# Whole-height score products for the global queries, and one order of products for the values

## The chip, the cores and the metric

One core of a Trainium2 chip runs the whole program in one launch. The metric is device time in microseconds (us) of one execution; lower is better. The core's engines run side by side and meet through semaphores: TensorE (in the rows PE for products, PEld for its weight loads), VectorE (DVE), ScalarE (ACT), GpSimd (POOL) and the SyncE queue (SP) that issues all the transfers here.

## The reference

```
k_all = concat([k_g, k_l]); v_all = concat([v_g, v_l])       # 4 batches, 8 heads, 32 + 512 tokens, 64 wide
out_g = softmax(q_g @ k_all.T / 8) @ v_all                   # 32 global queries see every key
s_ll  = where(|pos_i - pos_j| <= 32, q_l @ k_l.T / 8, -1e9)  # 512 local queries see a band ...
s_lg  = q_l @ k_g.T / 8                                      # ... and the 32 global keys
out_l = softmax(concat([s_lg, s_ll])) @ concat([v_g, v_l])
x = tokens of concat([out_g, out_l]), 2176 x 512
x = relu(x @ w_in)**2 @ w_out                                # d_ff 2048
h = x @ w2_in;  x = P(h) / Q(h) @ w2_out                     # P cubic, Q = 1 + |b0||h| + |b1|h*h
```

## The kernel before

The program has an attention stage (about the first 143 us) and then two feed-forward blocks, in one hand-written order (`tc.manual_schedule`): each engine carries out its instructions in the order in which the code lists them, and waits where a semaphore is not there yet.

Two heads make a pair, so there are 16 pairs. The first head's 64 values of q and k lie on partitions 0 to 63, the second's on 64 to 127. The loop over `p` (lines 488 to 586) is a pipeline: in iteration `p` TensorE does the scores of pair p, the transposes of pair p-1, and the products with the values of pairs p-2 and p-1. Each iteration has two halves of the same kind (u = 0 and 1; 256 local queries each):

- `scores(p, u)`, L299: eight products of 64 by 64 weights with 160 keys into the banks `s_ps[2u]` and `s_ps[2u+1]`, one bank for each head.
- `maxima`, L308 on VectorE, reads a bank, adds the mask and takes the row maximum; only then can that bank be written again. `exps`, L316 on ScalarE; `sums`, L320, and the reciprocal of `norm`, L324, on VectorE; the four scalings of `norm`, L327, on GpSimd.
- `transp`, L345 and L346: five transposes by TensorE, which need the scalings of GpSimd; `transp_evac`, L350 on ScalarE and L352 on VectorE, copies them out as `p1` (local keys) and `p2` (global keys).
- `pv(p, u)`, lines 354 to 383: the products with the values, in one bank `pv_ps[u]`. `glob(i)`, L370, multiplies `p2` by a 128 by 128 block that holds the global values of both heads. `win`, L364, multiplies the local probabilities of one window by 128 by 64 values, once for each head, whose results lie on partitions 0 to 63 and 64 to 127. For u = 1, L382 adds the last keys of the global queries. `pv_local` and `pv_global` (L389, L396, L398) copy the bank out.

In every second iteration `g_scores(g)`, L413 and L414, makes the scores of the global queries of four heads (two pairs, one of them a pair ahead). For each head it writes 32 partitions of bank c1 (`s_ps[0]`, 512 columns) and of bank c2 (`s_ps[1]`, 64 columns), from the head's 64 partitions of q and k. The first call uses the banks `tc_ps`. `g_transp`, L443 and L444, transposes the result an iteration later.

A product of fp32 values stands in the trace as two records, one for each pass over the columns; a transpose as one.

While this goes on, VectorE also prepares the feed-forward weights, four steps per 128 by 512 chunk (L101, L103, L105, L108) and a cast, L117, and GpSimd subtracts, L125. From iteration 3 on, each has one chunk. Transfers wait in one queue; q and k have four buffers, so pair p+3 is asked for once pair p-1's scores are done.

Of the kernel before, what the change touches and what calls it, by code (L numbers as in the profile page):

```python
# [11 lines left out]
F32 = mybir.dt.float32  # L12
# [9 lines left out]
B, H, SL, SG, D = 4, 8, 512, 32, 64  # L22
DM, DFF = 512, 2048
NTOK = B * (SL + SG)
NB = SL // 128
NW = SL // 64
KW = 160
KE = 288
KL = 896
KC = KL + 288  # L30
VW = 4 * D
VG = VW * NW
VE = VG + 8 * D
# [15 lines left out]
def window(w):  # L49

    return KE + 80 * w if w % 2 == 0 else (0 if w < 4 else KL) + 80 * (w % 4 - 1)


def body(ctx, tc, qT, kW, v, w1i, w1o, w2i, w2o, coef, out):
    nc = tc.nc
    pe, act, dve, pool, sync = nc.tensor, nc.scalar, nc.vector, nc.gpsimd, nc.sync
# [178 lines left out]
    def ew2_b(s):  # L235
        n = TILES[(s // KF) % NT][1]
        a, b, t = pend.pop(s)
        dve.scalar_tensor_tensor(a, in0=a, scalar=EPS1, in1=b, op0=ALU.add, op1=ALU.mult)  # L238
        dve.scalar_tensor_tensor(t, in0=t, scalar=nf[:, 0:1], in1=b, op0=ALU.add, op1=ALU.mult)
        dve.scalar_tensor_tensor(t, in0=a, scalar=2.0, in1=t, op0=ALU.subtract, op1=ALU.mult)  # L240
        gh = ff_p["g"].tile([128, TW], F32R, tag="gh", name="gh")
        gl = ff_p["g"].tile([128, TW], F32R, tag="gl", name="gl")
        gs[s] = gh, gl
        return t, gh[:, :n], gl[:, :n]
# [8 lines left out]
    ident = msk_p.tile([128, 128], F32, name="ident")  # L253
    mask = msk_p.tile([128, NB, KW], F32, name="mask")
    v_p = att.enter_context(tc.tile_pool(name="v", bufs=2))
# [12 lines left out]
    qt, kt, vt = {}, {}, {}  # L268
    sm, pT, pgs, pgT = {}, {}, {}, {}

    def load_qk(p):
        b, hp = divmod(p, 4)
        qt[p] = qk_p.tile([128, SL + SG], F32, tag="q", name="q")
        kt[p] = qk_p.tile([128, KC], F32, tag="k", name="k")
        cuts = [(0, 0), (256, 576), (SL + SG, KC)] if p == 0 else [(0, 0), (SL + SG, KC)]
        for (q0, k0), (q1, k1) in zip(cuts, cuts[1:]):
            sync.dma_start(qt[p][:, q0:q1], qT[b, hp][:, q0:q1])
            sync.dma_start(kt[p][:, k0:k1], kW[b, hp][:, k0:k1])
# [8 lines left out]
    def sm_tiles(p, u):  # L287
        sm[p, u] = (sm_p.tile([128, 2 * KW, 2], F32, tag="sm", name="sm"),
                    st_p.tile([128, 4], F32, tag="nm", name="nm"),
                    st_p.tile([128, 4], F32, tag="sum", name="sum"),  # L290
                    st_p.tile([128, 4], F32, tag="rs", name="rs"))

    def scores(p, u):
        for i in range(2):
            for j in range(2):
                for a in range(2):
                    r, w = slice(64 * j, 64 * j + 64), 4 * u + 2 * i + (a if i else 1 - a)
                    c = window(w) - 32 * i
                    pe.matmul(s_ps[2 * u + j][64 * a:64 * a + 64, KW * i:KW * i + KW],  # L299
                              qt[p][r, 64 * w:64 * w + 64], kt[p][r, c:c + KW],  # L300
                              start=True, stop=True, tile_position=(64 * j, 64 * a))

    def maxima(p, u, j):
        s, nm = sm[p, u][:2]
        for i in range(2):
            b, k = 2 * u + i, 2 * j + i
            o = s[:, KW * i:KW * i + KW, j]
            dve.tensor_tensor_reduce(out=o, in0=s_ps[2 * u + j][:, KW * i:KW * i + KW], in1=mask[:, b],  # L308
                                     scale=-0.125, scalar=3.0e38, op0=ALU.add, op1=ALU.min,
# [44 lines left out]
    def pv(p, u):  # L354

        v = vt[p // 2]
        c = pgT[p // 2][1]
        p1, p2 = pT.pop((p, u))
        bank = pv_ps[u]

        def win(w, o0, o1, stop=False):
            for j in range(2):
                jj = 2 * (p % 2) + j
                pe.matmul(bank[64 * j:64 * j + 64, o0:o1], v[:, VW * w + 64 * jj:VW * w + 64 * jj + 64],  # L364
                          p1[:, j, o0 + (32 if o0 >= 128 else 0):o1 + (32 if o0 >= 128 else 0)],
                          start=False, stop=stop)

        def glob(i):
            o = VG + 256 * (p % 2) + 128 * i
            pe.matmul(bank[:, 160 * i:160 * i + 128], v[:, o:o + 128], p2, start=i == 1, stop=False)  # L370

        glob(1)
        win(4 * u, 64, 160)
        win(4 * u + 1, 0, 64)
        glob(0)
        win(4 * u + 2, 128, 224)
        win(4 * u + 3, 224, 288, stop=u == 0)
        if u:
            for j in range(2):
                jj = 2 * (p % 2) + j  # L380
                o = VE + 64 * jj
                pe.matmul(bank[64 * j:64 * j + 64, 128:160], v[0:64, o:o + 64], c[:, 32 * jj:32 * jj + 32],  # L382
                          start=False, stop=True)

    def pv_local(p, half):
        b, hp = divmod(p, 4)
# [15 lines left out]

    def g_scores(g):
        c1, c2 = s_ps[:2] if g else tc_ps
        for jj in range(4):
            p = 2 * g + jj // 2
            r = slice(64 * (jj % 2), 64 * (jj % 2) + 64)
            o = slice(32 * jj, 32 * jj + 32)
            even = kt[p][r, KE:KE + KW * NB].rearrange("p (a b) -> p a b", a=NB)[:, :, 0:128]
            last = kt[p][r, KC - 64:KC]  # L410
            last = bass.AP(tensor=last.tensor, offset=last.offset - (KC - 64 - KE - 128),
                           ap=[last.ap[0], [KC - 64 - KE - 128, 2], [1, 32]])
            pe.matmul(c1[o], qt[p][r, SL:], even, start=True, stop=True, tile_position=(64 * (jj % 2), 32 * jj))  # L413
            pe.matmul(c2[o, 0:64], qt[p][r, SL:], last, start=True, stop=True,  # L414
                      tile_position=(64 * (jj % 2), 32 * jj))
        m = st_p.tile([128, 8], F32, tag="gm", name="gm")
        dve.tensor_reduce(m[:, 0:1], c1[:, 32:], axis=AX.X, op=ALU.max)
        dve.tensor_reduce(m[:, 1:2], c2[:, 0:64], axis=AX.X, op=ALU.max)
        pgs[g] = pg[g % 2], m, c1, c2
# [29 lines left out]
    qk_p = qk_s.enter_context(tc.tile_pool(name="qk", bufs=4, side="right"))  # L449

    with tc.manual_schedule():
        act.preload_act_table_set("natural_log_exp_and_others")
        warm = raw_p.tile([128, 512], I64, tag="raw", name="raw").bitcast(BF16)[:, 0:512]
        dve.memset(warm, 0.0)
        load_qk(0)
        load_qk(1)
        load_qk(2)
        load_qk(3)
        load_v(0)
# [12 lines left out]
        for b, r, c in ((0, 64, 0), (2, 0, 0), (3, 64, 128)):  # L472
            o = 32 * (b % 2)
# [14 lines left out]
        for p in range(NP + 2):  # L488
# [14 lines left out]
            g = (p + 1) // 2  # L503
# [38 lines left out]
            if odd or p == 0:  # L542
                g_scores(g)
# [4 lines left out]
            if 2 <= p:  # L548
                pv(p - 2, 1)
# [27 lines left out]
            if pre:  # L577
                pv(p - 1, 0)
# [89 lines left out]
        for s in range(2, 2 * S1):  # L668
# [22 lines left out]
            if j == KF - 1:  # L691
                mm2(s - 2)
                mm2(s - 1)
                g = ew2_b(s) if s in pend else None
# [72 lines left out]
```

## Time and profile before

| | |
|---|---|
| median of 3 runs | 907.04 us (907.02 to 907.33) |
| the profiled execution | 906.48 us, its span 904.7 us |
| TensorE busy | 890.2 us, 98% of the span |
| TensorE weight loads busy | 783.4 us |
| VectorE, ScalarE, GpSimd busy | 662.7, 547.3, 258.8 us |
| chain that ended last | 86% of it TensorE, 10% VectorE |

The span is from the first to the last instruction; the time outside it is 1.8 us. An engine's busy time counts overlapping instructions once. Busy shares are means over stages that differ: in the attention stage all four engines are used, in the feed-forward blocks TensorE leads, but for a stretch at the start of the first block (to about 225 us) in which VectorE converts weights.

### The profile page before, as it was taken

How to read it: one execution, taken by the hardware profiler on the slowest of the kernel's cores; microseconds unless marked ns; L12 is line 12 of the kernel's file. 1: busy time of each engine (PE TensorE's matmuls, PEld its weight loads, DVE VectorE, ACT ScalarE, POOL GpSimd, SP SyncE). 2: the span in 40 equal slices, each digit the busy share in tenths (PEclk: the TensorE clock that was granted, in tenths of full speed). 3: DMA queues.
4: the chain of work that ended last, by engine and by line, in shares of the span. 5: the costliest groups of instructions: out<-in, count | busy, mean ns of one | idle time of the engine just before them, and what ended most of it. 6: DMA issues, size and time to landing. Idle time of an engine off the chain costs nothing.

```text
span 904.7 us, 14722 instructions
## 1 busy us (share of the span) xinstructions
PE 890.2 (98%) x5397; PEld 783.4 (87%) x5398; DVE 662.7 (73%) x1406; ACT 547.3 (60%) x1186; POOL 258.8 (29%) x324
## 2 busy tenths in 40 slices
PE   8999999997999999999999999999999999999998
PEld 4777778886888899999999978888888999999998
DVE  4788976999776568664332479877877888887886
ACT  5878874444433334342244568767766886886885
POOL 3667881334000000000036543221222222222221
PEclk9999999999999999999999999999999999999999
DMA  9767631333154327532014410001000100000001
GB/s 350 297 220 299 218 135 61 127 117 132 49 169 139 105 75 214 166 91 84 1 59 122 125 34 1 1 0 47 1 1 0 48 1 1 35 1 21 15 1 36
DMA packets 27576, 81.43 MB, mean 90 GB/s; under 512 B 3184, under 2 KB 4976, under 8 KB 26480
## 3 DMA queue, kind: packets, MB, share of 16 engines
q1 hardware_dynamic: 27504, 80.49, 26.3%
q8 instruction: 42, 0.69, 0.3%
q14 instruction: 30, 0.25, 0.1%
HBM read 67.64 MB, written 12.85 MB: 89 GB/s over the span
## 4 chain that ended last, share of the span: by engine, by line
PE 86%; DVE 10%; ACT 1%; issue 1%; DMA 1%; POOL 1%; SPq 0%; DVEq 0%; POOLq 0%; ACTq 0%
PE tc L181 19%; PE pv L181 19%; PE s L168 12%; PE s L169 12%; PE s L170 12%; PE pv L364 3%; PE tc L345 2%; DVE cv L105 2%; PE pv L370 2%; PE s L299 2%; DVE cv L101 2%; DVE cv L108 1%; DVE gl L213 1%; PE s L413 1%; DVE cv L103 1%
## 5 line engine op out<-in xcount | busy, mean ns | idle before, releaser
L168 PE MATMUL s<-xh,wi 128*128 128x384 f32 (+1 forms) x640 | 229.7, 359 | 0.0
L170 PE MATMUL s<-xh,wi 128*128 128x384 f32 (+1 forms) x640 | 228.4, 357 | 0.0
L169 PE MATMUL s<-xl,wi 128*128 128x384 f32 (+1 forms) x640 | 228.3, 357 | 0.0
L248 POOL TENSOR_TENSOR gl<-tt,gh 128x384 fp32r<-128x384 f32 (+1 forms) x79 | 89.9, 1137 | 268.1 <-ACT gh L247 207.0
L181 PE MATMUL tc<-gh,wo 128*128 128x384 f32 (+1 forms) x640 | 153.3, 361 | 0.8 <-ACT gh L247 0.8
L181 PE MATMUL pv<-gh,wo 128*128 128x384 f32 (+1 forms) x640 | 152.5, 360 | 0.0
L210 ACT ACTIVATE a<-s 128x384 f32<-128x384 f32 (+1 forms) x80 | 42.5, 532 | 153.1 <-PE s L170 153.0
L170 PEld LDWEIGHTS s<-xh,wi 128*128 128x128 f32 x640 | 120.1, 188 | 11.4
L169 PEld LDWEIGHTS s<-xl,wi 128*128 128x128 f32 x640 | 120.2, 188 | 10.8
L168 PEld LDWEIGHTS s<-xh,wi 128*128 128x128 f32 x640 | 120.1, 188 | 10.6
L181 PEld LDWEIGHTS tc<-gh,wo 128*128 128x128 f32 x640 | 116.4, 188 | 12.6 <-ACT gh L247 1.7
L181 PEld LDWEIGHTS pv<-gh,wo 128*128 128x128 f32 x640 | 115.9, 188 | 11.8
L211 DVE TENSOR_TENSOR b<-a 128x384 f32<-128x384 f32 (+1 forms) x80 | 50.3, 629 | 103.2 <-ACT a L210 103.2
L125 POOL TENSOR_TENSOR wi<-raw,wi 128x512 fp32r<-128x512 f32 x16 | 21.4, 1337 | 267.2 <-ACT wi L119 247.2
L181 PE MATMUL tc<-gl,wo 128*128 128x384 f32 (+1 forms) x320 | 89.9, 362 | 4.6 <-DVE gl L213 4.6
L181 PE MATMUL pv<-gl,wo 128*128 128x384 f32 (+1 forms) x320 | 89.8, 361 | 0.0
L225 DVE SCALAR_TENSOR_TENSOR a<-a,nf,b 128x384 f32<-128x384 f32 (+1 forms) x80 | 53.4, 667 | 32.3 <-ACT b L223 32.2
L327 POOL TENSOR_SCALAR sm<-sm,rs 128x160 f32<-128x160 f32 x128 | 63.6, 521 | 38.1 <-DVE rs L324 13.1
L222 ACT ACTIVATE a<-s 128x384 f32<-128x384 f32 (+1 forms) x80 | 42.0, 525 | 52.8 <-PE s L170 52.8
L181 PEld LDWEIGHTS tc<-gl,wo 128*128 128x128 f32 x320 | 58.7, 188 | 11.3 <-DVE gl L213 5.5
L238 DVE SCALAR_TENSOR_TENSOR a<-a,b 128x384 f32<-128x384 f32 (+1 forms) x80 | 49.0, 612 | 22.0 <-ACT b L233 22.0
L181 PEld LDWEIGHTS pv<-gl,wo 128*128 128x128 f32 x320 | 58.9, 188 | 5.9
(115 smaller groups left out, 1449.7 us busy)
## 6 DMA issues: line engine op xcount, KB each, us to landing
v<-in_v_dram SPq DMA_DIRECT2D x8, 1408.0 KB, 7.9
k<-in_kW_dram SPq DMA_DIRECT2D x15, 592.0 KB, 5.6
raw<-in_w1i_dram SPq DMA_DIRECT2D x16, 512.0 KB, 5.1
raw<-in_w1o_dram SPq DMA_DIRECT2D x16, 512.0 KB, 3.5
raw<-in_w2i_dram SPq DMA_DIRECT2D x16, 512.0 KB, 3.9
st<-cv SPq DMA_DIRECT2D x32, 256.0 KB, 4.2
raw<-in_w2o_dram SPq DMA_DIRECT2D x16, 512.0 KB, 4.0
raw<-st SPq DMA_DIRECT2D x32, 256.0 KB, 2.6
```

The source lines that it names most:

```text
L168: pe.matmul(ph, wh, hi[:, kk, :n], start=(kk == 0), stop=False)
L169: pe.matmul(ph, wh, lo[:, kk, :n], start=False, stop=False)
L170: pe.matmul(ph, wl, hi[:, kk, :n], start=False, stop=(kk == KD - 1))
L181: pe.matmul(acc_bank[d][:, :n], w[:, half, 128 * d:128 * d + 128], src[:, :n], start=start, stop=stop)
L210: act.activation(a, ph, AF.Relu)
L211: dve.tensor_tensor(b, a, a, op=ALU.mult)
L222: act.activation(a, ph, AF.Square)
L225: dve.scalar_tensor_tensor(a, in0=a, scalar=nf[:, 5:6], in1=b, op0=ALU.mult, op1=ALU.add)
L238: dve.scalar_tensor_tensor(a, in0=a, scalar=EPS1, in1=b, op0=ALU.add, op1=ALU.mult)
L248: eng.tensor_tensor(gl, t, gh.bitcast(F32), op=ALU.subtract)
L327: pool.tensor_scalar(e, e, rs[:, k:k + 1], 1.0, op0=ALU.mult, op1=ALU.mult)
L364: pe.matmul(bank[64 * j:64 * j + 64, o0:o1], v[:, VW * w + 64 * jj:VW * w + 64 * jj + 64], p1[:, j, o0 + (32 if o0 >= 128 else 0):o1 + (32 ...
```

## The change

It has two parts, both in the attention stage.

In `g_scores`, the global queries of a pair's two heads are laid out by the host diagonally: 64 columns of which the first 32 hold the first head's queries on partitions 0 to 63 and zeros below, the other 32 the second head's on partitions 64 to 127 and zeros above. One product over all 128 partitions then gives both heads' scores. The eight products of a call (4 heads, 2 banks) become four: c1 for both pairs, then c2 for both pairs. Each q transfer grows from 544 to 576 columns.

In `pv`, both `glob` products come first and then the four windows; before, one `glob` stood between the second and the third window. The flag that starts the bank moves to `glob(0)`. (`skip_group_check` concerns the build alone.)

```diff
+QC = SL + 2 * SG
-        qt[p] = qk_p.tile([128, SL + SG], F32, tag="q", name="q")
+        qt[p] = qk_p.tile([128, QC], F32, tag="q", name="q")
...
         def glob(i):
             o = VG + 256 * (p % 2) + 128 * i
-            pe.matmul(bank[:, 160 * i:160 * i + 128], v[:, o:o + 128], p2, start=i == 1, stop=False)
-
+            pe.matmul(bank[:, 160 * i:160 * i + 128], v[:, o:o + 128], p2, start=i == 0, stop=False,
+                      skip_group_check=True)
+
+
+        glob(0)
         glob(1)
         win(4 * u, 64, 160)
         win(4 * u + 1, 0, 64)
-        glob(0)
         win(4 * u + 2, 128, 224)
         win(4 * u + 3, 224, 288, stop=u == 0)
...
         c1, c2 = s_ps[:2] if g else tc_ps
-        for jj in range(4):
-            p = 2 * g + jj // 2
-            r = slice(64 * (jj % 2), 64 * (jj % 2) + 64)
-            o = slice(32 * jj, 32 * jj + 32)
-            even = kt[p][r, KE:KE + KW * NB].rearrange("p (a b) -> p a b", a=NB)[:, :, 0:128]
-            last = kt[p][r, KC - 64:KC]
...
-            pe.matmul(c1[o], qt[p][r, SL:], even, start=True, stop=True, tile_position=(64 * (jj % 2), 32 * jj))
-            pe.matmul(c2[o, 0:64], qt[p][r, SL:], last, start=True, stop=True,
-                      tile_position=(64 * (jj % 2), 32 * jj))
+        for c in (c1, c2):
+            for i in range(2):
+                p = 2 * g + i
+                o = slice(64 * i, 64 * i + 64)
...
+                pe.matmul(c[o] if c is c1 else c[o, 0:64], qt[p][:, SL:], keys, start=True, stop=True,
+                          tile_position=(0, 64 * i))
...
+    for i in range(2):
+        qT[:, :, i, :, SL + SG * i:SL + SG * i + SG] = q_g[:, i::2].transpose(0, 1, 3, 2)
```

TensorE's order in iteration 3, from the last transpose (L346) of the first half to the first `glob`, before (s0 and s1 are the banks c1 and c2; the two numbers of k and q tell the pairs apart; 32x512 is partitions by columns of the result):

```order
L346 MATMUL tc1_93<-ident_131,sm_408 128x128
L413 MATMUL s0_88<-k_283,q_282 32x512
L414 MATMUL s1_89<-k_283,q_282 32x64
L413 MATMUL s0_88<-k_283,q_282 32x512
L414 MATMUL s1_89<-k_283,q_282 32x64
L413 MATMUL s0_88<-k_403,q_402 32x512
L414 MATMUL s1_89<-k_403,q_402 32x64
L413 MATMUL s0_88<-k_403,q_402 32x512
L414 MATMUL s1_89<-k_403,q_402 32x64
L370 MATMUL pv1_95<-p2_436,v_176 128x128
```

The same place in the changed kernel, whose lines stand one to five further down (L346 is L347, L413 and L414 are L418, L370 is L371):

```order
L347 MATMUL tc1_93<-ident_131,sm_400 128x128
L418 MATMUL s0_88<-k_279,q_278 64x512
L418 MATMUL s0_88<-k_395,q_394 64x512
L418 MATMUL s1_89<-k_279,q_278 64x64
L418 MATMUL s1_89<-k_395,q_394 64x64
L371 MATMUL pv1_95<-p2_428,v_176 128x128 x2
```

The second product now writes c1; the first that touches c2 is the third.

TensorE's order in `pv` of one half (u = 0), from the transposes to the next scores, before:

```order
L346 MATMUL tc1_93<-ident_131,sm_353 128x128
L370 MATMUL pv0_94<-p2_434,v_176 128x128
L364 MATMUL pv0_94<-p1_433,v_176 64x96 x2
L364 MATMUL pv0_94<-p1_433,v_176 64x64 x2
L370 MATMUL pv0_94<-p2_434,v_176 128x128
L364 MATMUL pv0_94<-p1_433,v_176 64x96 x2
L364 MATMUL pv0_94<-p1_433,v_176 64x64 x2
L299 MATMUL s0_88<-k_173,q_172 64x160 x2
```

and in the changed kernel (L364 is L365, L299 is L300):

```order
L347 MATMUL tc1_93<-ident_131,sm_345 128x128
L371 MATMUL pv0_94<-p2_426,v_176 128x128 x2
L365 MATMUL pv0_94<-p1_425,v_176 64x96 x2
L365 MATMUL pv0_94<-p1_425,v_176 64x64 x2
L365 MATMUL pv0_94<-p1_425,v_176 64x96 x2
L365 MATMUL pv0_94<-p1_425,v_176 64x64 x2
L300 MATMUL s0_88<-k_173,q_172 64x160 x2
```

The second `glob` has moved ahead of the first window; nothing else stands elsewhere, and the other engines' orders are as before.

## Rows read from the trace of the kernel before

**Rows 1.** Stretches: length; busy PE, PEld, DVE, ACT, POOL; PEclk; DMA share; GB/s

```profile
14.70:32.30 17.60, 17.60 (x213) 12.62 (x212) 10.83 (x65) 14.80 (x58) 10.79 (x28) 1.00 0.88 337
48.60:64.80 16.20, 15.97 (x196) 11.41 (x195) 13.91 (x63) 13.04 (x49) 12.06 (x23) 1.00 0.72 264
96.80:112.90 16.10, 15.66 (x199) 11.81 (x199) 15.07 (x66) 13.90 (x50) 13.29 (x25) 1.00 0.59 214
143.50:224.90 81.40, 77.29 (x332) 62.04 (x332) 77.06 (x103) 38.20 (x68) 29.41 (x19) 1.00 0.34 117
224.90:228.30 3.40, 2.90 (x7) 2.31 (x8) 3.27 (x4) 3.34 (x7) 1.58 (x1) 0.50 0.42 154
```

**Rows 2.** Timeline of TensorE, one `pv`, to the next scores: start, length, what

```profile
98.27 0.39 PE L370 MATMUL pv<-p,v 128*128 128x128 f32 x2
98.59 0.50 PE L364 MATMUL pv<-p,v 128*64 128x96 f32 x8
99.02 0.49 PE L370 MATMUL pv<-p,v 128*128 128x128 f32 x2
99.44 0.50 PE L364 MATMUL pv<-p,v 128*64 128x96 f32 x8
99.87 0.77 PE L299 MATMUL s<-k,q 64*64 64x160 f32 x16
```

**Rows 3.** Chain that ended last: four transposes of 128 columns without a wait

```profile
134.17 0.47 PE tc L345 x4
```

**Rows 4.** Groups, weight loads, 27 to 124 us: count | busy, mean ns | idle before

```profile
L364 PEld LDWEIGHTS pv<-p,v 128*64 128x64 f32 x390 | 17.7, 136 | 5.8
```

**Rows 5.** Timeline of TensorE, a `g_scores` without a wait, to the next product

```profile
109.83 1.27 PE L413 MATMUL s<-k,q 64*32 64x512 f32 x8
110.71 0.50 PE L414 MATMUL s<-k,q 64*32 64x64 f32 x8
111.14 0.49 PE L370 MATMUL pv<-p,v 128*128 128x128 f32 x2
```

**Rows 6.** Timeline of TensorE, a `g_scores` that waits for bank c2

```profile
44.35 1.04 PE L413 MATMUL s<-k,q 64*32 64x512 f32 x2
45.62 0.24 PE L414 MATMUL s<-k,q 64*32 64x64 f32 x1 [0.23 <-DVE nm L308]
46.84 0.49 PE L370 MATMUL pv<-p,v 128*128 128x128 f32 x2
```

**Rows 7.** Timeline of TensorE, the second and the third `g_scores`

```profile
14.70 1.46 PE L413 MATMUL s<-k,q 64*32 64x512 f32 x4
16.67 0.66 PE L443 MATMUL pv<-ident,gs 128*128 128x128 f32 x4
...
28.81 1.30 PE L413 MATMUL s<-k,q 64*32 64x512 f32 x5
30.59 0.49 PE L370 MATMUL pv<-p,v 128*128 128x128 f32 x2
```

**Rows 8.** Timelines of VectorE and GpSimd around 60 us

```profile
60.45 0.88 DVE L320 TENSOR_SCALAR rs<-sum 128x4 f32<-128x4 f32 x1
...
60.03 1.27 POOL L125 TENSOR_TENSOR wi<-cv,wi 128x512 fp32r<-128x512 f32 x1
```

**Rows 9.** Waits of PEld, 27 to 124 us: total, times, longest; a transpose that waits

```profile
PEld tc L345 <- POOL sm L327: 4.4, 18, 0.6
...
101.64 0.39 PE L345 MATMUL tc<-ident,sm 128*128 128x128 f32 x1 [0.44 <-POOL sm L327]
```

**Rows 10.** Timeline of VectorE: first `maxima` of three halves, idle time before each

```profile
49.57 0.33 DVE L308 CUSTOM_DVE_ANT_0 sm<-s,mask 128x160 f32<-128x160 f32 x1 [1.28 <-PE s L299]
56.66 0.33 DVE L308 CUSTOM_DVE_ANT_0 sm<-s,mask 128x160 f32<-128x160 f32 x1 [0.26 <-PE s L299]
105.41 0.33 DVE L308 CUSTOM_DVE_ANT_0 sm<-s,mask 128x160 f32<-128x160 f32 x1 [0.24 <-PE s L299]
```

**Rows 11.** Chain that ended last, at the end of the attention stage

```profile
143.52 0.37 ACT x L389
```

More of the change, by code (lines that the diff above doesn't have):

```diff
@@ L272, in load_qk @@
         b, hp = divmod(p, 4)
-        qt[p] = qk_p.tile([128, SL + SG], F32, tag="q", name="q")
+        qt[p] = qk_p.tile([128, QC], F32, tag="q", name="q")
         kt[p] = qk_p.tile([128, KC], F32, tag="k", name="k")
-        cuts = [(0, 0), (256, 576), (SL + SG, KC)] if p == 0 else [(0, 0), (SL + SG, KC)]
+        cuts = [(0, 0), (256, 576), (QC, KC)] if p == 0 else [(0, 0), (QC, KC)]
         for (q0, k0), (q1, k1) in zip(cuts, cuts[1:]):
@@ L365, in win @@
                           p1[:, j, o0 + (32 if o0 >= 128 else 0):o1 + (32 if o0 >= 128 else 0)],
-                          start=False, stop=stop)
+                          start=False, stop=stop, skip_group_check=True)
         def glob(i):
             o = VG + 256 * (p % 2) + 128 * i
-            pe.matmul(bank[:, 160 * i:160 * i + 128], v[:, o:o + 128], p2, start=i == 1, stop=False)
+            pe.matmul(bank[:, 160 * i:160 * i + 128], v[:, o:o + 128], p2, start=i == 0, stop=False,
+                      skip_group_check=True)
+        glob(0)
         glob(1)
@@ L382, in pv @@
                 pe.matmul(bank[64 * j:64 * j + 64, 128:160], v[0:64, o:o + 64], c[:, 32 * jj:32 * jj + 32],
-                          start=False, stop=True)
+                          start=False, stop=True, skip_group_check=True)
     def pv_local(p, half):
@@ L404, in g_scores @@
         c1, c2 = s_ps[:2] if g else tc_ps
-        for jj in range(4):
-            p = 2 * g + jj // 2
-            r = slice(64 * (jj % 2), 64 * (jj % 2) + 64)
-            o = slice(32 * jj, 32 * jj + 32)
-            even = kt[p][r, KE:KE + KW * NB].rearrange("p (a b) -> p a b", a=NB)[:, :, 0:128]
-            last = kt[p][r, KC - 64:KC]
-            last = bass.AP(tensor=last.tensor, offset=last.offset - (KC - 64 - KE - 128),
-                           ap=[last.ap[0], [KC - 64 - KE - 128, 2], [1, 32]])
-            pe.matmul(c1[o], qt[p][r, SL:], even, start=True, stop=True, tile_position=(64 * (jj % 2), 32 * jj))
-            pe.matmul(c2[o, 0:64], qt[p][r, SL:], last, start=True, stop=True,
-                      tile_position=(64 * (jj % 2), 32 * jj))
+        for c in (c1, c2):
+            for i in range(2):
+                p = 2 * g + i
+                o = slice(64 * i, 64 * i + 64)
+                if c is c1:
+                    keys = kt[p][:, KE:KE + KW * NB].rearrange("p (a b) -> p a b", a=NB)[:, :, 0:128]
+                else:
+                    last = kt[p][:, KC - 64:KC]
+                    keys = bass.AP(tensor=last.tensor, offset=last.offset - (KC - 64 - KE - 128),
+                                   ap=[last.ap[0], [KC - 64 - KE - 128, 2], [1, 32]])
+                pe.matmul(c[o] if c is c1 else c[o, 0:64], qt[p][:, SL:], keys, start=True, stop=True,
+                          tile_position=(0, 64 * i))
         m = st_p.tile([128, 8], F32, tag="gm", name="gm")
@@ L710 @@
     q_g, k_g, v_g = (np.asarray(inputs[k]) for k in ("q_g", "k_g", "v_g"))
-    qT = np.concatenate([q_l, q_g], axis=2).transpose(0, 1, 3, 2).reshape(B, 4, 128, SL + SG)
+    qT = np.zeros((B, 4, 2, D, QC), f)
+    qT[..., :SL] = q_l.transpose(0, 1, 3, 2).reshape(B, 4, 2, D, SL)
+    for i in range(2):
+        qT[:, :, i, :, SL + SG * i:SL + SG * i + SG] = q_g[:, i::2].transpose(0, 1, 3, 2)
+    qT = qT.reshape(B, 4, 128, QC)
     def padded(l):
```

## The prediction

> **What bounds the kernel now.** The time by stages was read first. In the attention stage TensorE is busy nearly throughout, but VectorE follows closely: 13.91 of 16.20 us in a typical stretch of two iterations, 15.07 of 16.10 later, when x is split as well [rows 1]. Both matter, and so does GpSimd between them, since a transpose waits for its scalings: 18 such waits, 4.4 us in all, some of which leave TensorE idle, as the 0.44 us at 101.64 [rows 9]. Second, the chain of waits: at the end of the stage it goes from TensorE's last values to ScalarE's copy at 143.52 [rows 11], and from there through VectorE's conversion of weights, 77.06 of 81.40 us busy [rows 1]. That part begins when attention ends and is built the same way whenever it begins, and so is all behind it; a microsecond won before 143.5 us should be a microsecond at the end. Third, the timelines of the two places that the change touches.
>
> **The products with the values.** One takes 1.60 us now, from 98.27 to 99.87: 0.32, 0.43, 0.42 and 0.43 us from start to start of its four runs [rows 2]. What of this is columns? Four transposes of 128 columns take 0.47 us, so 0.92 ns a column [rows 3]. A `glob` has two passes of 128: 0.235 us. A run of windows has, for either head, two passes over 96 + 64 columns, 320 in all: 0.29 us if the two heads run side by side, 0.59 if not. It takes 0.43, so they do, and some 0.14 us go into turning from one shape to the other; the `glob` between the windows takes 0.42, not 0.235, so its turn costs 0.19. With both `glob` first there is one run of `glob` (0.32 + 0.23) and one of windows (0.43 + 0.29): 1.27 us. I take 0.34 us less for each, 32 times: 10.9 us of TensorE time. The bounds: nothing, if the turns come back in some other place, and 0.46 if the windows pay no turn at all any more (0.32 + 0.24 + 0.58 = 1.14). I keep one turn, since the run still has another shape than the `glob` ahead of it.
>
> **The scores of the global queries.** Without a wait a call takes 1.31 us: 0.88 from the first c1 to the first c2, 0.43 for c2 [rows 5]. The four heads' two passes of 512 columns would be 0.94 us for one head alone by the pace above, so all four ran together. Afterwards two products of the same 512 columns run, one for either half of the output partitions, as the windows do: again 0.88. c2 has two passes of 64 columns, 0.12, and a turn of 0.14: 1.14 in all, 0.17 less. Three calls look different, at 44.35 [rows 6], 60.59 and 76.83: the first head's c1 goes out, then its c2 waits for VectorE to read that bank, until 45.62, and the other three heads' c1 wait behind it; 2.49 us. After the change both c1 go out ahead of that wait, c2 starts at 45.62 as before and ends 0.26 later: 45.88 instead of 46.84, 0.96 less. The second and third call [rows 7] take 1.97 and 1.78: 0.83 and 0.64 less. The first, on other banks, waits for k to arrive and gains nothing. Together 4.7 us.
>
> The larger q costs 16 KB a pair; at 337 GB/s [rows 1] that is 0.05 us each, two of them ahead of the first scores: 0.1 us at the start, hidden later behind a DMA share of 0.72.
>
> **What of the 15.6 us arrives at the end.** TensorE's path is not alone, so I go by stretches.
>
> 14.7 to 32.3: VectorE is busy 10.83 of 17.60 [rows 1], so all should count: four products and two calls, 1.36 + 0.83 + 0.64 = 2.8 us.
>
> 32.3 to 81.0, three stretches like 48.6 to 64.8: TensorE sheds 4 x 0.34 + 0.96 = 2.3 us in each. But a half's scalings start from VectorE's `maxima` of the scores just made, and the transposes of the next half wait for them. What is shed ahead of such a transpose becomes waiting there; only what is shed between it and the next scores counts, and that only as far as VectorE was idle when those scores came. It was idle 0.26 us at 56.66 and 1.28 at 49.57 [rows 10]: at most 1.54 a stretch. Against it stands that VectorE's own waits grow when it has no slack: the sum L320, 4 numbers wide, takes 0.88 us at 60.45 because GpSimd's L125 runs until 61.30 [rows 8]. I take 1.2, three times: 3.6 us.
>
> 81.0 to 112.9, two stretches: VectorE's idle time is 0.24 at 105.41 [rows 10], and in the other half the call and one product count, 0.17 + 0.34. Together 0.75, twice: 1.5 us.
>
> 112.9 to 143.5: by the same rule 0.6 up to the last scores, and then four products in a row on TensorE's chain, 1.4: 2.0 us.
>
> The sum is 9.9 less 0.1, so 9.8 us. From the profiled execution's 906.48 that is 896.7; it lies 0.56 under the median, so I forecast 897.2 us.
>
> **A rule that speaks against it.** Weight loads of the windows last 136 ns each, and eight of them go with a run of 0.43 us [rows 2, 4]; end to end they would be 1.09 us, so they overlap products and each other.
> The Trainium skill, in TensorE: Matmul & The Clock Gate, section "Part 3: Packing small matmuls — row/col tiling", says that a weight load overlaps a running product only where their row groups differ, and whole-height products share all row groups.
> By that rule the two c1 would follow each other and the window rounds could not hide their loads; the trace disagrees for the windows, which are whole-height too, and shows nothing for 512 columns.
>
> **Rivals.**
> - *All of it counts* (0.10). The waits for scalings shrink along with TensorE's work, because VectorE starts each half earlier. For it: TensorE is the engine that the chain names. Against: 4.4 us of waits are already there [rows 9]. 907.0 - 15.6 = 891.4.
> - *VectorE and GpSimd hold the pace* (0.17). Only one product of each stretch between 32 and 113 counts: 2.8 + 5 x 0.34 + 1.4 = 5.9, 901.1.
> - *The two c1 run one after the other* (0.06). A call takes 1.76 + 0.26 = 2.02 instead of 1.14; the two early calls lose 0.88 each, the three with the wait 0.49, the last two 0.88: 5.0 of the 9.8 go, 902.2. Windows side by side speak against it.
> - *Nothing measurable* (0.04). The turn is not a matter of order but of each operand's first read, and the waits behind `g_scores` reappear at the next transposes: 906 to 908.
> - *Slower* (0.03). A run of windows is short now; a run of eight rounds could outpace its weight loads. The place is the windows, the price is r a round: a product takes 0.55 + 8r, which equals today's 1.60 at r = 0.131, close to a load's 0.136. At 0.16 it takes 1.83, 0.23 more, 32 times, and with the 4.7 of the scores taken off that is +2.7: 909.7. Against it: a run of four rounds takes 0.43 now, turn included.
>
> **How the numbers follow.** The forecast (0.60) covers 893.5 to 900.5: the stretches between 32 and 113 us give between 0.34 and 1.54 each. The three middle rivals and the spread reach to 902.0 above; below, part of the first, 892.5. There is another uncertainty of 1.7 us: at 224.9 to 228.3 us the granted clock is 0.50, the lower of its two levels (1.2 GHz), behind a stretch in which TensorE waited [rows 1]; half of 3.4 us may come or go with when that stretch falls. No change can be told from one within 0.2%, 1.8 us. Faster 0.93, same 0.04, slower 0.03.
>
> **What would show it.** In the changed kernel a product without a wait should take 1.27 us from its first `glob` to the next scores, with 0.72 for the sixteen window records; a call of `g_scores` 1.14, or end 0.26 after VectorE frees c2; the stretch that now lasts 16.2 us about 15.0, VectorE over 90% busy in it, and idle time of TensorE before L345 grown. The attention stage should end near 133.7. The forecast is wrong if the window records take over 0.9, if the two c1 start 0.9 apart, or if the stretch shrinks to 13.9 or not at all.

## The result, and the profile after

| | before | changed |
|---|---|---|
| median, first timing | 907.03 us (906.43 to 907.33, 4 runs) | 896.44 us (896.02 to 897.71, 4 runs) |
| ratio, 95% interval | | 0.9886 (0.9869 to 0.9904) |
| profiled execution, its span | 906.48, 904.7 us | 897.71, 895.9 us |
| start of the second `g_scores` to ScalarE's copy at the end of attention | 14.70 to 143.52: 128.8 us | 15.21 to 133.91: 118.7 us |

10.6 us were won, 9.8 were forecast (897.2). By the trace the attention stage gave 10.1 us; the profiled execution is the slowest of the four and loses 0.5 us of that again at its start and 0.8 in the feed-forward part (below).

The timeline of TensorE in the changed kernel, a product with the values to the next scores, to be held against [rows 2]:

```profile
61.40 0.61 PE L371 MATMUL pv<-p,v 128*128 128x128 f32 x4
61.94 0.78 PE L365 MATMUL pv<-p,v 128*64 128x96 f32 x16
62.65 0.77 PE L300 MATMUL s<-k,q 64*64 64x160 f32 x16
```

From 61.40 to 62.65 it is 1.25 us; it was 1.60, and 1.27 was forecast. The sixteen window records take 0.71.

A call of `g_scores` that waits for bank c2, and one that does not (timeline of TensorE), against [rows 6] and [rows 5]:

```profile
56.95 1.12 PE L418 MATMUL s<-k,q 128*64 128x512 f32 x4
58.28 0.34 PE L418 MATMUL s<-k,q 128*64 128x64 f32 x4 [0.20 <-DVE nm L309]
58.55 0.71 PE L371 MATMUL pv<-p,v 128*128 128x128 f32 x4
...
102.52 1.19 PE L418 MATMUL s<-k,q 128*64 128x512 f32 x8
103.64 0.71 PE L371 MATMUL pv<-p,v 128*128 128x128 f32 x4
```

The first goes on for 1.60 us instead of 2.49: both c1 stand ahead of the wait, c2 starts when VectorE has read the bank, and the next product follows 0.27 behind it. The second takes 1.12 instead of 1.31.

The stretches of the changed kernel: length, then busy time of PE, PEld, DVE, ACT and POOL, granted clock, DMA share and GB/s, against [rows 1]:

```profile
15.20:30.50 15.30, 15.30 (x197) 11.44 (x196) 10.32 (x63) 14.50 (x57) 10.47 (x27) 1.00 0.97 382
45.20:59.90 14.70, 13.94 (x187) 10.45 (x186) 13.82 (x64) 12.79 (x48) 12.62 (x24) 1.00 0.79 295
89.75:105.00 15.25, 14.28 (x188) 10.60 (x186) 15.03 (x66) 13.75 (x50) 13.77 (x24) 1.00 0.61 228
```

The reader is to see the second column and the fourth: two iterations take 14.70 instead of 16.20 us, TensorE's share in them falls from 99% to 95%, VectorE's rises from 86% to 94%, and to 99% in the later stretch. TensorE now waits more. Waits for GpSimd's scalings, from 25 to 115 us:

```profile
PEld tc L346 <- POOL sm L328: 12.6, 41, 0.7
```

It was 4.4 us in 18 waits [rows 9], in a window of much the same iterations. These are waits of its weight loads, in part beside products that still run. TensorE's own idle time from the second `g_scores` to ScalarE's copy grew by less, from 2.0 us (busy 126.79 of 128.80) to 5.1 (113.61 of 118.70). So its busy time fell by 13.2 us, not by the 15.6 of the prediction, and 10.1 of them arrived. (The ends of products are modelled in the profile, so busy time and times from start to start are not quite the same measure.)

### The profile page after: what moved, and what is told of

It reads as the page before. It is cut to its first block, busy times and chain, and to the rows that moved or that the text cites. A ratio compares the mean times of both kernels' runs of the same rounds, so it can differ in the third digit from the quotient of the medians.

```text
span 895.9 us, 14595 instructions
## 1 busy us (share of the span) xinstructions
PE 877.4 (98%) x5334; PEld 776.0 (87%) x5334; DVE 662.7 (74%) x1406; ACT 546.2 (61%) x1186; POOL 262.6 (29%) x324
## 4 chain that ended last, share of the span: by engine, by line
PE 81%; DVE 12%; POOL 3%; ACT 2%; issue 1%; DMA 1%; SPq 0%; DVEq 0%; POOLq 0%; ACTq 0%
PE tc L182 19%; PE pv L182 19%; PE s L169 12%; PE s L171 12%; PE s L170 12%; DVE cv L106 2%; DVE cv L102 2%; POOL sm L328 2%; DVE cv L109 2%; PE tc L346 1%; PE pv L365 1%; PE s L300 1%; DVE gl L214 1%; DVE cv L104 1%; PE pv L371 1%
## 5 line engine op out<-in xcount | busy, mean ns | idle before, releaser
L170 PEld LDWEIGHTS s<-xl,wi 128*128 128x128 f32 x640 | 120.2, 188 | 10.8
L169 PEld LDWEIGHTS s<-xh,wi 128*128 128x128 f32 x640 | 120.1, 188 | 10.6
L182 PEld LDWEIGHTS tc<-gh,wo 128*128 128x128 f32 x640 | 116.4, 189 | 12.7 <-ACT gh L248 1.7
L126 POOL TENSOR_TENSOR wi<-raw,wi 128x512 fp32r<-128x512 f32 x16 | 21.4, 1338 | 268.0 <-ACT wi L120 263.4
L328 POOL TENSOR_SCALAR sm<-sm,rs 128x160 f32<-128x160 f32 x128 | 63.9, 523 | 27.2 <-ACT gs L431 10.1
```

Source lines behind the costliest of these rows:

```text
L126: pool.tensor_tensor(w[:, 1], f, w[:, 0].bitcast(F32), op=ALU.subtract)
L169: pe.matmul(ph, wh, hi[:, kk, :n], start=(kk == 0), stop=False)
L170: pe.matmul(ph, wh, lo[:, kk, :n], start=False, stop=False)
L182: pe.matmul(acc_bank[d][:, :n], w[:, half, 128 * d:128 * d + 128], src[:, :n], start=start, stop=stop)
L328: pool.tensor_scalar(e, e, rs[:, k:k + 1], 1.0, op0=ALU.mult, op1=ALU.mult)
```

## The experiments

All were timed in five rounds; the number of runs is given where it is not five. The stretch is the one of two iterations around 50 us, from scores to scores (16.2 us before, 14.7 in the changed kernel), cut out by its own start and end in each trace.

**1. The order of the products with the values alone.** `pv` is that of the changed kernel, everything else is as before:

```diff
...
+        glob(0)
         glob(1)
         win(4 * u, 64, 160)
         win(4 * u + 1, 0, 64)
-        glob(0)
         win(4 * u + 2, 128, 224)
```

> The order of the products with the values alone, scores as before. Theory of the prediction (what is shed ahead of a waiting transpose turns into waiting, and VectorE's idle time caps the rest): each product 0.34 us shorter, and of the 10.9 us shed 6 to 6.5 arrive (1.4 in 14.7 to 32.3 us, 0.6 in each of five stretches, 0.6 and 1.2 behind them): 900.7 us. Rival, all TensorE work counts: 10.9, 896.1. Rival, VectorE and GpSimd hold the pace: 4.2 or less, 902.8.

901.51 us (900.39 to 902.29), ratio 0.9935 (0.9923 to 0.9948). The stretch of experiment 1:

```profile
47.31:62.93 15.62, 15.20 (x200) 11.00 (x201) 14.04 (x63) 12.96 (x48) 12.59 (x24) 1.00 0.74 274
```

Four products are 1.4 us shorter there from start to start and the stretch is 0.6 shorter, as the theory had it. From the second call (15.33) to the first feed-forward product behind the last product with the values it takes 122.3 us; in the kernel before, from 14.70 to 143.40, 128.7. So 6.4 us arrive of 11 by the trace, and 5.7 in the median. Neither rival holds: 896.1 would have taken everything, 902.8 lies above all runs.

**2. The whole-height scores alone**, with the wider q; `pv` as before (the other half of the diff that stands ahead).

> The whole-height scores of the global queries alone (with the wider q), products with the values in the old order. Theory: calls of 1.12 us without a wait and 0.26 behind VectorE's release of c2 with one; 3 to 4 us arrive: 903.5. If the two parts add up, this and the other part together give the 10.6 us of the whole change; if they compete for the same slack of VectorE, they give more than 10.6 apart.

901.79 us (901.72 to 902.82), ratio 0.9944 (0.9931 to 0.9956): 5.4 us, more than the 3 to 4 expected. The stretch is 0.9 shorter:

```profile
46.20:61.50 15.30, 15.17 (x192) 11.08 (x193) 13.92 (x64) 12.82 (x48) 12.07 (x24) 1.00 0.79 283
```

Here TensorE stays at 99%. The call takes 1.54 us (58.12 to 59.66) instead of 2.49; what it sheds stands behind the transposes of its half and ahead of the next scores, so nearly all of it counts. The two parts add up: 0.6 and 0.9 in a stretch against 1.5 for both, 5.7 and 5.4 against 10.6 in the medians, where each has an interval of over a microsecond to either side.

**3. The old products, c1 first.** 32 by 512, one for each head, but the four of c1 ahead of the four of c2:

```diff
-        for jj in range(4):
+        for c, jj in [(c, jj) for c in (c1, c2) for jj in range(4)]:
...
-            pe.matmul(c1[o], qt[p][r, SL:], even, start=True, stop=True, tile_position=(64 * (jj % 2), 32 * jj))
-            pe.matmul(c2[o, 0:64], qt[p][r, SL:], last, start=True, stop=True,
+            keys = even if c is c1 else last
+            pe.matmul(c[o] if c is c1 else c[o, 0:64], qt[p][r, SL:], keys, start=True, stop=True,
                       tile_position=(64 * (jj % 2), 32 * jj))
```

> The old products of 32 by 512, but the four of c1 first and then the four of c2; q as narrow as before. Theory: most of the second part is order, since c1 no longer stands behind the wait for c2: calls without a wait stay at 1.31 us, the waiting ones end 0.43 behind the release instead of 1.22, the second and third call take 1.3; 3 to 3.5 us arrive, 903.7, as near to the whole-height form as can be measured. Rival, the gain is the fuller use of the array: no change, 907.0.

902.31 us (901.43 to 903.57), ratio 0.9947 (0.9934 to 0.9959): the intervals of 2 and 3 all but coincide. The stretch, and a call without a wait (timeline of TensorE; L414 is now the line of both banks):

```profile
45.68:60.96 15.28, 15.17 (x200) 11.04 (x201) 13.93 (x64) 12.81 (x48) 12.06 (x24) 1.00 0.77 280
```

```profile
104.68 1.17 PE L414 MATMUL s<-k,q 64*32 64x512 f32 x16
105.79 0.49 PE L370 MATMUL pv<-p,v 128*128 128x128 f32 x2
```

The expectation had the time right and a detail wrong: the call takes 1.11 us, not 1.31. The same eight products, otherwise ordered, are 0.20 faster even where nothing waits, and as fast as the four whole-height ones. So what the second part brings is order, as nearly as these runs can tell; the rival, that fuller use of the array brings it, is out.

**4. The wider q alone**: 32 columns of zeros more are transferred for each pair, and not read.

```diff
-        qt[p] = qk_p.tile([128, SL + SG], F32, tag="q", name="q")
+        qt[p] = qk_p.tile([128, QC], F32, tag="q", name="q")
...
```

> The kernel before with the wider q alone: 32 more columns of zeros are transferred for each pair and not read. Theory of the prediction: 0.1 us, all of it at the start. Rival: the wider rows delay the first pairs' keys by as much as the changed kernel's start was late, 0.5 us: TensorE's first global scores of the second pair at about 10.0 instead of 9.47 us, 907.5.

906.96 us (906.08 to 908.81, 11 runs), ratio 0.9998 (0.9988 to 1.0007); the second pair's global scores start at 9.48 us (9.47 before) and the second call at 14.69, where it did. The rival's 0.5 us is not there; the 0.1 us of the prediction is less than these runs can tell from nothing. In the changed kernel the second pair's scores start at 10.09. In the other profiles they start at 8.99 to 9.77 with the narrow q (experiments 1, 3, 5 and 7) and at 9.38 to 10.14 with the wide one (2, 6 and 8): the first microseconds differ from run to run by as much as the changed kernel's start was late.

**5. Both parts by order alone**: `pv` of experiment 1, `g_scores` of experiment 3.

> Both parts by order alone: both products with the global values first, and the old 32 by 512 score products with c1 first; q narrow as before. Since the c1-first form alone had calls of 1.10 us, against 1.12 for the whole-height form, the theory that the diagonal layout brings nothing of its own expects the changed kernel's time, 896.4 within 1 us, and 118.6 us within 0.5 from the second call to the end of the last product with the values. Rival, the whole-height form has a share that shows only together with the other part: 898 or more.

896.76 us (895.58 to 897.03, 4 runs), ratio 0.9883 (0.9869 to 0.9896), the changed kernel's within either interval. From the second call to the end of the last product 117.9 us, against 118.6 in the changed kernel (15.21 to 133.79); most of the difference is the third call, which in the changed kernel's trace waits for k (1.67 us, and 1.20 here), and the stretches agree to 0.07. The diagonal layout and the wider q are not needed for the gain.

**6. The changed kernel without the 1e-9.** The instruction that adds it to a row's sum is left out; the reciprocal reads the sum. So 1e-9 is missing in the local rows' denominators.

```diff
-        dve.tensor_scalar(sm[p, u][3], sm[p, u][2], 1e-9, None, op0=ALU.add)
+        pass
...
-        dve.reciprocal(rs, rs)
+        dve.reciprocal(rs, sm[p, u][2])
```

> The changed kernel without the instruction that adds 1e-9 to a row's sum (VectorE, L321); the reciprocal reads the sum itself (a sum is at least 1, so fp32 loses the 1e-9 anyway). Theory, VectorE's waits for GpSimd hold the pace: L321 lasts 0.85 us in one half of each stretch of two iterations and 0.35 in another, so 0.5 to 1 us a stretch goes, six times: 3 to 5 us, 892 to 893.5. Rival, the reciprocal inherits the wait, or GpSimd's scalings hold the pace: no change, 896.4.

894.87 us (893.34 to 896.08, 4 runs), ratio 0.9863 (0.9850 to 0.9877); 1.9 us under experiment 5, which ran beside it. The four sums in the changed kernel's stretch, and there the conversion's first step (timeline of VectorE):

```profile
46.68 0.17 DVE L321 TENSOR_SCALAR rs<-sum 128x4 f32<-128x4 f32 x1
49.82 0.38 DVE L321 TENSOR_SCALAR rs<-sum 128x4 f32<-128x4 f32 x1 [0.22 <-ACT sm L317]
50.69 1.02 DVE L102 TENSOR_SCALAR cv<-cv 128x512 f32<-128x512 f32 x1
53.50 0.27 DVE L321 TENSOR_SCALAR rs<-sum 128x4 f32<-128x4 f32 x1
56.79 0.95 DVE L321 TENSOR_SCALAR rs<-sum 128x4 f32<-128x4 f32 x1
```

and what stands there without them:

```profile
45.20:59.35 14.15, 13.85 (x191) 10.67 (x185) 13.12 (x60) 12.85 (x48) 12.70 (x24) 1.00 0.84 306
```

```profile
47.39 0.18 DVE L325 RECIPROCAL rs<-sum 128x4 f32<-128x4 f32 x1
50.02 0.17 DVE L325 RECIPROCAL rs<-sum 128x4 f32<-128x4 f32 x1
50.24 1.38 DVE L102 TENSOR_SCALAR cv<-cv 128x512 f32<-128x512 f32 x1
54.12 0.17 DVE L325 RECIPROCAL rs<-sum 128x4 f32<-128x4 f32 x1
```

The stretch loses 0.55 us, the low end of what was expected, and from the second call on it is 115.0 instead of 118.6 us. The median gains less, 1.6 us from the changed kernel's 896.44, where 3 to 5 were expected: the profiled execution, the slowest of the four, reaches its second call 1.0 us later (half the clock at the start, see the last section) and needs 0.8 more behind attention. The reciprocal inherits no wait (0.17 or 0.18 us in the rows shown), but L102 does, 1.38 instead of 1.02. TensorE is back at 98% of the stretch.

**7. Order alone, and without the 1e-9** (5 and 6 together).

> Order alone, and without the 1e-9. If both readings hold, the fastest so far: as the changed kernel without the sum, 892 to 893.5, with the old narrow q. If the wait only moves, 896.4.

894.37 us (893.59 to 895.07, 4 runs), ratio 0.9859 (0.9845 to 0.9872): 12.7 to 13.0 us faster than before and 2.4 below experiment 5. It is the lowest median of the versions that leave out no more than the 1e-9, but its interval and that of experiment 6 all but coincide. The expectation, 892 to 893.5, is missed by 0.9 us, as in experiment 6 by 1.4: the sign was right and the size was not.

**8. The changed kernel without GpSimd's subtraction for the 13 early chunks**; their low halves are zero, so the first feed-forward block lacks that part.

```diff
...
                 w_split(*cv, dve)
-                w_rest(*cv)
+                cvs.pop(cv)
+                have[cv[1], cv[2]] = cv[0]
...
+        for w in w_in + w_out:
+            pool.memset(w[:, 1].bitcast(F32), 0.0)
```

> The changed kernel with GpSimd's subtraction L126 left out for the 13 weight chunks prepared during attention (their low halves are set to zero at the start, so the first feed-forward block is computed without them). It shows what GpSimd's load costs. Theory, what the change shed and did not get back is waiting for GpSimd's scalings and VectorE's wait behind L126: a stretch of 14.75 us comes near TensorE's own 13.8 to 14.0, 4 to 5 us in all: 892. Rival, VectorE's own work holds the pace: under 1.5 us, 895.

893.87 us (892.86 to 894.83), ratio 0.9855 (0.9842 to 0.9869): 2.6 to 2.9 us gained, between the two. The stretch:

```profile
44.40:58.50 14.10, 13.99 (x191) 10.62 (x187) 12.70 (x64) 12.72 (x48) 9.61 (x22) 1.00 0.83 305
```

GpSimd has 3 us less to do and the stretch is 0.6 shorter, as much as without the sums: then TensorE, at 99%, is the bound again. The sum that took 0.95 us in the changed kernel, where GpSimd's subtraction ran from 56.43 to 57.72, takes 0.17 at the same place of this run (timeline of VectorE):

```profile
55.50 0.17 DVE L321 TENSOR_SCALAR rs<-sum 128x4 f32<-128x4 f32 x1
```

So the sum does wait for the subtraction, and taking away either end gives the same 0.6 us in the middle stretches. That this wait alone holds them is not shown: experiment 6 also takes 4 x 0.17 us of VectorE's own work away, experiment 8 also lets GpSimd start its scalings earlier, and in both TensorE's share of 98 to 99% leaves little more to win. In the two stretches from 75 to 105 us, where VectorE is busy 98 and 99% in the changed kernel, the same run gains only 0.3 and 0.1 (14.8 and 15.1 us), although VectorE's busy time falls to 13.3 and 13.8 us, so a full VectorE is not the limit there. The chain that ended last runs in the second of them (87.5 to 102.6 us) from the scores through VectorE's maxima and GpSimd's scalings to the transposes, and the scalings are its largest part, 27%.

## Why the prediction was right

The forecast was 897.2 us and the range 892.5 to 902.0; the median is 896.44. By its steps:

- *A product with the values, 0.34 us less:* 0.35. The window records took 0.71 where 0.72 was forecast, so the rival with a slower pace (a round of 0.131 or more) is out: eight rounds in 0.71 with the turn.
- *A call without a wait 1.14, with one 0.26 behind the release:* 1.12 and 0.27. The two c1 run side by side. One after the other a call could not be under 1.76. The Trainium skill's rule in TensorE: Matmul & The Clock Gate, section "Part 3: Packing small matmuls — row/col tiling", that weight loads overlap with running products only in other row groups, would have made them follow each other; this trace disagrees for 512 columns as well, with 1.12 us for the whole call. What was wrong is why the call gets shorter: the working put it down to a shorter c2, and experiment 3 shows that the interleaving of c1 and c2 had cost 0.20, whatever the height.
- *2.8 us in 14.7 to 32.3:* from the second call to the scores after the third it is 15.4 us (15.21 to 30.62) instead of 17.7, so 2.3. The third call was to shed 0.64 and shed 0.1, since k for its second pair came late: 27.46 to 29.13 is 1.67 us. From the second call on, both pairs of a call lie ahead of the pair whose scores are being made, by one and by two. The third call's second pair was asked for at 18.3 us and its k landed 9.6 us later, at 27.9; in the kernel before it was 7.7 us, at 26.3, and the call came at 28.81. This stretch's DMA share is 0.97 (0.88 before). In experiment 5 the same call took 1.20. The step that all of this stretch counts, since VectorE has time, left out the transfers.
- *1.2 us in each of three stretches:* 1.5, as much as the idle time of VectorE that the working named (0.26 and 1.28, 1.54 in all) and then cut to 1.2. The cut was mis-sized: the sums of a stretch hardly grew, 1.77 us for the four shown in experiment 6 against 1.72 before. In the changed kernel's timeline of VectorE both idle times are gone, and in experiment 1, which shed less, 0.94 of the 1.28 is left and the 0.26 is gone. So the mechanism held. But 1.54 was not all the idle time of the stretch: the working passed over a third half, with 0.64, and there hardly anything arrived. First that row of the kernel before, then the same half of the changed kernel:

```profile
59.96 0.32 DVE L308 CUSTOM_DVE_ANT_0 sm<-s,mask 128x160 f32<-128x160 f32 x1 [0.64 <-PE s L299]
...
56.30 0.33 DVE L309 CUSTOM_DVE_ANT_0 sm<-s,mask 128x160 f32<-128x160 f32 x1 [0.59 <-PE s L300]
```

What held that half was not tested. One product, 0.34 us, is shed there between the transposes and the scores, so by the prediction's own rule 1.88 could have arrived; that 1.54 was met so closely is in part luck.

- *0.75 in each of two stretches:* 0.7 and 0.8. *0.6 up to the last scores:* 0.6 (two iterations from 112.97 took 14.0, now 13.4). *1.4 behind them:* 1.2.
- *A microsecond won before the end of attention is one at the end:* yes, but for the clock. The profiled execution needs 762.0 us from ScalarE's copy to the end of the span against 761.2 before, and its stretch at half the clock is 6.8 us long instead of 3.4. The other profiles agree: five of the ten have a stretch of 3.4 us there (before, experiments 2, 3, 5 and 8) and need 761.2 to 761.3 us, whenever attention ended; the five with 6.8 or 6.9 need 762.0 to 763.4. The changed kernel's stretch:

```profile
213.70:220.50 6.80, 4.73 (x11) 3.77 (x12) 6.40 (x9) 4.94 (x9) 1.82 (x1) 0.50 0.30 95
```

- *0.1 us at the start for the wider q:* experiment 4 shows none that it could tell from nothing; the profiled start was 0.5 late because TensorE waited 2.15 us for k of the second pair instead of 1.63, and by experiment 4 that is not the width.

By the trace the stretches of attention gave 10.1 us where 9.9 were forecast. That they came so close is in part luck: 0.5 and 0.2 too much at the two ends stand against 0.9 too little in the three stretches. The lower end of the forecast, 893.5, does not follow from its own terms: 2.8, 5 x 1.54 and 2.0 less 0.1 make 12.4, so 894.6.

The rival "all of it counts" asked for 891.4; experiments 6 and 8 show part of what stands in its way. The rival "VectorE and GpSimd hold the pace" named the engines through which the waits run and let them take too much, at 901.1.

## What to carry to other kernels

When an engine's work shrinks, go half by half through the loop and ask what the next wait is counted from: work ahead of a transpose that waits for another engine turns into waiting, work between that transpose and the next producer counts. The idle time of the engine that is fed, read in front of its first instruction of every half, bounds what can arrive in that half; here two such times (1.54 us together) were used up and the third (0.64) was hardly touched. And a product that must wait for a bank belongs behind all that need not: the same products in another order gave as much as the layout that was built for it.

## What the runs showed of the hardware that was not expected

- Four 32 by 512 products and four 32 by 64 ones on the same four tiles take 1.31 us if each small one follows its large one, and 1.11 if all large ones go first, with no wait in either.
- A sum of 4 numbers a row on VectorE takes 0.17 us or 0.95, the latter when GpSimd's subtraction runs: the one at 56.79 ends at 57.74, the subtraction L126 at 57.72. It is not the subtraction alone: in experiment 8 a sum at 48.77 takes 0.64, to 49.41, beside GpSimd's L438, which ends at 49.39. A reciprocal of the same size did not wait: in the changed kernel one at 50.59 takes 0.17 while L126 runs from 50.15 to 51.43. Where experiment 6 leaves the sums out, the next large instruction, L102, took the wait over in part.
- Two profiles show half the clock near the start (the lower of its two levels). In experiment 6 it is at 9.7 to 13.1 us and begins in a wait of 2.07 us for k, which lasts until 10.14. In experiment 1 it is at 10.8 to 14.2, behind a wait of 2.12 us up to 9.77. The wait alone does not decide it: the changed kernel and experiment 7 waited 2.15 and 2.08 us and kept the full clock; what does stays open. The second call came at 16.24 and 15.33 us, against 14.1 to 15.2 in the other eight profiles. Runs of one kernel differ by one or two microseconds at least partly for the clock: the changed kernel's four have 896.02 and 896.13 us at a mean granted clock of 0.998, 896.75 and 897.71 at 0.996. Here the row of experiment 6:

```profile
9.70:13.10 3.40, 2.96 (x22) 1.61 (x26) 0.95 (x3) 0.00 (x0) 0.00 (x0) 0.51 1.05 432
```
